# An mLSTM with a channel-mix layer: the hand-ordered list of steps is replaced, with more idle matmuls and a taller spread

## The chip, the cores and the metric

The kernel runs on one core of one Trainium2 chip. The metric is the device time of one execution in microseconds (us). Four compute engines take part: PE (TensorE, matmuls), DVE (VectorE), ACT (ScalarE) and POOL (GpSimd); the SP queue issues every DMA. Each engine works through its own queue strictly in the order in which the program lists its instructions, and waits at an instruction until what it needs is there.

## The reference

There are 4 batches, 8 heads, 768 steps in time and 40 values per head. First an mLSTM recurrence with running maxima `m` as stabilisers runs over the time steps:

```python
m_new = np.maximum(f_gate[:, :, t] + m, i_gate[:, :, t])
f_stab = np.exp(f_gate[:, :, t] + m - m_new); i_stab = np.exp(i_gate[:, :, t] - m_new)
C = f_stab * C + i_stab * (v_t outer k_t);  n = f_stab * n + i_stab * k_t
y[t] = sigmoid(o_gate[t]) * (C @ q_t) / max(|n . q_t|, 1)
```

The heads are then joined to x (4 x 768 x 320), and a channel mix follows, with a shift by one step in time:

```python
xk = mu_k * x + (1 - mu_k) * x_prev;  xr = mu_r * x + (1 - mu_r) * x_prev
out = sigmoid(xr @ w_r) * (np.maximum(xk @ w_k, 0)**2 @ w_v)     # w_k 320x1024, w_v 1024x320
```

## The kernel before, in words

The time axis is cut into 6 chunks of 128 steps, and two batches make a pair. One chunk of one pair is a unit; there are 12 units (u = 0 to 11, chunk u // 2), each with two halves i (one per batch). The recurrence is worked in its chunked form: inside a chunk as a masked attention, between chunks by the state C.

For one half of a unit: `scores` (L268, 16 matmuls) gives k.q in PSUM; `exps` (L257, ACT, four per call) makes the decay weights e; `weigh` (L273, DVE) multiplies the two; `carry_in` (L279) scales k for the state; `attend` (L313, PE) multiplies with v and with the old state; `carry_add` (L323, L325, DVE) updates C; `norm` (L335, L337, L339, three small DVE instructions called den), `gate` (L344) and `outcome` (L350) make x; `twin`, `turn` (L362, PE) and `turned` (L369, ACT) turn it so that channels lie on rows. Then for the whole unit: `change` and `mix` (L377, L383) form the shifted mixtures, `mix_h` and `mix_l` (L392, L398) split them into a rounded part and a remainder, `ffn_k` (L457, four calls of 16 matmuls), `relu`, `square`, `square_h`, `square_l` (L463 to L484), `ffn_r` (L491) and `ffn_v` (L513) do the products, and `result` and `store` finish.

The exponents need, for a given step in time, the running maximum of each head in all 128 rows. For chunk 0 that is done by PE: `spread` (L229 to L233) first adds the causal mask (a 128-row bf16 matmul of 512 columns), and then for each of four heads multiplies a column of the identity, repeated, with the 32 rows (4 batches x 8 heads) of maxima; two such banks per half, four halves for units 0 and 1. For later chunks a DMA does it (`fetch_m`).

The weights arrive as 64-bit floats in 19 pieces (8 of w_k, 3 of w_r, 8 of w_v). For each piece: `load_w` (DMA into one of three stage buffers), `size` (L418, ACT), `bits` steps 0 to 2 (L425, L427, L429, all on DVE), `parts` (the rounded part, mostly ACT, L435) and `parts_l` (the remainder, L441, DVE or POOL). A stage buffer is free again after `bits` step 2. So the first part of the run carries two things at once: the conversion of 19 pieces and the first units.

`warm(n)` (L101) issues n idle bf16 matmuls of 128 rows and 512 columns on constant data; nothing reads them, and they wait for nothing but the fill of ones at the start. Since each engine keeps to its queue, a `warm` delays the PE work listed behind it.

All of these steps are written out one after the other in a list (from L523 on), with the engine as an argument where there is a choice (V = DVE, G = POOL, A = ACT, SY = SP's queue). The list fixes the order on every engine. A planner made it beforehand; in the file it is only the list.

Of the kernel before, what the change touches and what calls it, by code (L numbers as in the profile page):

```python
# [8 lines left out]
F32 = mybir.dt.float32  # L9
# [30 lines left out]
def mlstm_cmix_kernel(ctx: ExitStack, tc, kq, vk, og, gi, gf, wk, wr, wv, mu, pad, out):  # L40
# [556 lines left out]
    bits("wk", 4, 2)
    carry_in(0, 0, V)
    load_o(0, SY)
    spread(1, 0)  # L600
    weigh(0, 1, 0)
    weigh(0, 1, 1)
    attend(0, 0)
    norm(0, 0, 0)
    attend(0, 1)
    parts("wk", 2, A)
    load_w("wk", 6, SY)
    norm(0, 0, 1)
# [5 lines left out]
    gate(0, 0, V)
    norm(0, 1, 0)
    size("wk", 6)
    parts("wk", 4, A)
    zero_state(0, G)
    bits("wk", 6, 0)
    exps(1, 0, 1)  # L620
    carry_add(0, 0)
    size("wr", 0)
    norm(0, 1, 1)
    norm(0, 1, 2)
    parts_l("wk", 4, G)
    spread(1, 1)
# [21 lines left out]
    scores(1, 1)
    weigh(1, 0, 0)
    weigh(1, 0, 1)  # L650
    parts("wr", 0, A)
    load_v(1, SY)
    carry_in(1, 0, V)
    change(0, 0, G)
# [5 lines left out]
    attend(1, 0)  # L660
    fetch_m(2, 0, SY)
    mask(2, 0)
    weigh(1, 1, 1)
    load_o(1, SY)
    parts_l("wr", 0, V)
# [36 lines left out]
    parts_l("wv", 1, G)
    square(0, 0, A)
    load_w("wv", 2, SY)
    bits("wr", 1, 1)
    size("wv", 2)
    carry_in(1, 1, G)
    bits("wr", 1, 2)
    parts("wr", 1, A)
    square_l(0, 0, V)  # L710
    attend(1, 1)
    fetch_m(2, 1, SY)
    bits("wv", 2, 0)
    bits("wv", 2, 1)
    bits("wv", 2, 2)
    load_w("wr", 2, SY)
    mask(2, 1)
    exps(2, 0, 0)
    weigh(2, 0, 0)
    relu(0, 3)  # L720
    norm(1, 1, 0)
    ffn_k(0, 2)
    norm(1, 1, 1)
    size("wr", 2)
    norm(1, 1, 2)
    bits("wr", 2, 0)
    bits("wr", 2, 1)
    bits("wr", 2, 2)
    parts_l("wr", 1, V)
    ffn_k(0, 1)  # L730
    square_h(0, 3, A)
    mix_h(0, "r")
    parts("wv", 2, A)
    parts("wr", 2, A)
    square(0, 3, A)
    mix_l(0, "r", V)
# [20 lines left out]
    ffn_r(0, 1)
    turn(1, 0)
    turned(1, 0)
    load_w("wv", 5, SY)  # L760
    bits("wv", 3, 0)
    load_w("wv", 7, SY)
    bits("wv", 3, 1)
    bits("wv", 3, 2)
    parts("wv", 3, A)
    square(0, 2, A)
    load_w("wv", 4, SY)
    gate(1, 1, V)
# [19 lines left out]
    parts("wv", 5, A)
    parts_l("wv", 5, V)
    parts("wv", 4, A)  # L790
    ffn_v(0, 0, 0, 1)
    load_v(2, SY)
    twin(1, 1, G)
    turn(1, 1)
    ffn_v(0, 1, 0, 1)
    turned(1, 1)
# [5 lines left out]
    fetch_g(2, 1, SY)
    bits("wv", 7, 1)
    bits("wv", 7, 2)
    zeros(1, SY)
    parts("wv", 7, A)
    queries(2, 0, V)
    load_v(3, SY)
    carry_in(2, 0, V)
    ffn_v(0, 0, 1, 2)  # L810
    exps(2, 1, 1)
    ffn_v(0, 0, 2, 3)
    bits("wv", 6, 0)
    bits("wv", 6, 1)
    bits("wv", 6, 2)
    parts("wv", 6, A)
    parts_l("wv", 6, G)
    load_s(3, SY)
    change(1, 0, V)
    change(1, 1, V)  # L820
    mix(1, "k")
# [1017 lines left out]
```

## Time and profile before

| | |
|---|---|
| median of 3 runs | 343.21 us (341.57 to 343.29) |
| the profiled execution | 342.23 us, of it 340.4 us from the first to the last instruction |
| PE busy | 323.1 us (95%) |
| DVE busy | 263.2 us (77%) |
| ACT busy | 223.3 us (66%) |
| POOL busy | 105.5 us (31%) |
| mean granted PE clock | 0.964 of full |

Busy time of PE is modelled (matmuls overlap), so two matmuls' lengths add up to more than the time between their starts. Where a price per matmul is needed, it is better to subtract starts. The granted clock has two levels, 1.2 GHz (0.50) and 2.4 GHz (1.00). The column shows 1.00 until the first change that the trace records, between 32 and 33 us; the lengths of like instructions tell more.

### The profile page before, as it was taken

What the parts mean: (1) busy time and instruction counts of PE and PEld (TensorE: products, weight loads), DVE (VectorE), ACT (ScalarE), POOL (GpSimd) and SP (SyncE); (2) the same over time, 40 slices, a digit from 0 to 9 for tenths busy, and PEclk for the clock granted to TensorE, in tenths of its full rate; (3) what the DMA queues carried; (4) which work ended last, traced back from release to release, by engine and by line L of the source; (5) the groups of instructions that cost most, each with busy time, mean ns of one, the idle gap of its engine ahead of it and who ended that gap; (6) DMA issues with size and microseconds to landing.
All of it is one profiled execution on the core that took longest, in us unless ns stands there. A gap on an engine that the chain in (4) does not pass through costs nothing.

```text
span 340.4 us, 8826 instructions
## 1 busy us (share of the span) xinstructions
PE 323.1 (95%) x3504; PEld 303.4 (89%) x3504; DVE 263.2 (77%) x576; ACT 223.3 (66%) x488; POOL 105.5 (31%) x129
## 2 busy tenths in 40 slices
PE   6999995977999999999999999999999999999996
PEld 3877785867999998999999989999999999999995
DVE  6596999898799977899578798679798776665432
ACT  3756588665788737936969457785776776734442
POOL 2333321121053227162235342556317062320030
PEclk9999598795999999999999999999999999999999
DMA  6749536970370694172945644582668044010011
GB/s 224 241 145 264 168 117 213 274 229 12 95 194 14 183 239 146 44 238 67 244 126 166 189 132 135 141 224 85 154 188 242 5 144 155 3 40 0 2 39 39
DMA packets 25440, 47.29 MB, mean 139 GB/s; under 512 B 2632, under 2 KB 16264, under 8 KB 24440
## 3 DMA queue, kind: packets, MB, share of 16 engines
q1 hardware_dynamic: 25400, 46.74, 47.0%
q8 instruction: 27, 0.44, 0.6%
q14 instruction: 13, 0.11, 0.1%
HBM read 42.63 MB, written 4.10 MB: 137 GB/s over the span
## 4 chain that ended last, share of the span: by engine, by line
PE 54%; DVE 19%; DMA 7%; ACT 4%; issue 2%; SPq 1%; DVEq 0%; ACTq 0%
PE pk L457 18%; PE pv L513 17%; PE pI L313 7%; PE pr L491 6%; PE pS L268 4%; DVE xm L383 4%; DMA vk_sb<-vk 3%; DMA g<-eg 3%; DVE e L273 2%; PE pT L362 1%; DMA wst<-wv 1%; DVE g L246 1%; DVE wf L429 1%; DVE x L354 1%; DVE wf L427 1%
## 5 line engine op out<-in xcount | busy, mean ns | idle before, releaser
L457 PE MATMUL pk<-xlk,wkh 128*128 128x256 f32 x288 | 76.5, 282 | 0.6 <-DVE xlk L398 0.6
L513 PE MATMUL pv<-wvl,kh 128*128 128x320 f32 x192 | 60.2, 313 | 3.7 <-DVE wvl L441 2.8
L513 PE MATMUL pv<-wvh,kh 128*128 128x320 f32 x192 | 61.6, 321 | 0.4 <-ACT wvh L435 0.4
L513 PE MATMUL pv<-wvh,kl 128*128 128x320 f32 x192 | 60.3, 314 | 0.3 <-DVE kl L484 0.2
L463 ACT ACTIVATE rl<-pk 128x512 f32<-128x512 f32 x48 | 28.3, 590 | 42.9 <-PE pk L457 42.6
L457 PEld LDWEIGHTS pk<-xlk,wkh 128*128 128x128 f32 x288 | 55.0, 191 | 1.0 <-DVE xlk L398 1.0
L457 PE MATMUL pk<-xhk,wkh 128*128 128x256 f32 x192 | 55.4, 288 | 0.0
L457 PE MATMUL pk<-xhk,wkl 128*128 128x256 f32 x192 | 53.9, 281 | 0.0
L257 ACT ACTIVATE e<-e,acol 128x128 f32<-128x128 f32 x160 | 50.4, 389 | 1.9 <-POOL e L221 1.7
L273 DVE TENSOR_TENSOR e<-pS,e 128x512 f32<-128x512 f32 x48 | 32.0, 683 | 12.3 <-PE pS L268 10.8
L513 PEld LDWEIGHTS pv<-wvl,kh 128*128 128x128 f32 x192 | 36.5, 190 | 4.5 <-DVE wvl L441 3.4
L383 DVE SCALAR_TENSOR_TENSOR xm<-xd,mu_sb,xT 128x256 f32<-128x256 f32 x72 | 37.3, 575 | 3.6 <-POOL xd L377 3.2
L513 PEld LDWEIGHTS pv<-wvh,kh 128*128 128x128 f32 x192 | 36.4, 190 | 1.5 <-ACT wvh L435 0.8
L513 PEld LDWEIGHTS pv<-wvh,kl 128*128 128x128 f32 x192 | 36.5, 190 | 1.3 <-DVE kl L484 0.9
L457 PEld LDWEIGHTS pk<-xhk,wkh 128*128 128x128 f32 x192 | 36.9, 192 | 0.3
L457 PEld LDWEIGHTS pk<-xhk,wkl 128*128 128x128 f32 x192 | 36.8, 191 | 0.0
L221 POOL TENSOR_SCALAR_AFFINE_SELECT e<-e 128x1024 f32<-128x1024 f32 x20 | 25.5, 1277 | 34.9 <-DMA e<-nm 34.8
L479 DVE CAST kh<-kk 128x512 fp32r<-128x512 f32 x44 | 21.1, 483 | 16.9 <-ACT kk L469 16.8
L469 ACT ACTIVATE kk<-rl 128x512 f32<-128x512 f32 x48 | 29.7, 628 | 1.7 <-DVE kl L484 0.5
L268 PE MATMUL pS<-kq 40*128 40x128 f32 x384 | 30.2, 308 | 0.0
L313 PE MATMUL pI<-vk_sb,e 128*64 128x41 f32 x768 | 29.6, 241 | 0.5 <-DVE e L273 0.5
L313 PEld LDWEIGHTS pI<-vk_sb,e 128*64 128x64 f32 x768 | 26.8, 149 | 3.3 <-issue 1.2
(114 smaller groups left out, 692.9 us busy)
## 6 DMA issues: line engine op xcount, KB each, us to landing
e<-nm SPq DMA_DIRECT2D x20, 512.0 KB
vk_sb<-vk SPq DMA_DIRECT2D x12, 648.0 KB
kq<-kq SPq DMA_DIRECT2D x24, 320.0 KB
g<-eg SPq DMA_DIRECT2D x40, 128.0 KB
sg<-og SPq DMA_DIRECT2D x12, 320.0 KB
out<-sg SPq DMA_DIRECT2D x24, 160.0 KB
wst<-wk SPq DMA_DIRECT2D x8, 384.0 KB
wst<-wv SPq DMA_DIRECT2D x8, 320.0 KB
```

The lines of the kernel that those rows point to most:

```text
L221: G.affine_select(e, e, pattern=[[0, H], [1, L]], compare_op=ALU.is_ge, fill=NEG, base=0, channel_multiplier=-1)
L257: A.activation(e[:, h, :], src, AF.Exp, bias=acol[:, cc, b * H + h:b * H + h + 1])
L268: T.matmul(pS[j][:, p * L:(p + 1) * L], kq2[rw, 0, p, cs], kq2[rw, 1, p, cs], start=True, stop=True)
L273: V.tensor_tensor(ev, t["S", i, half].rearrange("p (h t) -> p h t", h=HH), ev, op=ALU.mult)
L313: T.matmul(*m, start=n < 2, stop=n >= len(mms) - 2, skip_group_check=True)
L383: V.scalar_tensor_tensor(xm[:, ct, :].rearrange("p (b t) -> p b t", b=NB), t["xd"][:, ct], mu_sb[:, "kr".index(nm), ct:ct + 1], xT[u % G2] ...
L457: T.matmul(pk[:, i * U:(i + 1) * U], ww[:, 2 * pr + i, ct * P:(ct + 1) * P], xx[:, ct, :], start=n == 0, stop=n == len(tl) - 1)
L463: A.activation(r, t["pk", pr], AF.Relu)
L469: A.activation(kk, t["r", pr], AF.Square)
L479: eng.tensor_copy(kh, t["kk", pr])
L491: T.matmul(pr[:, :DM], xx[:, ct, i * P:(i + 1) * P], ww[:, ct, :], start=m == 0, stop=m == len(tl) - 1)
L513: T.matmul(t["pv", i][:, :DM], xx[:, ts], ww[:, f, :], start=f == 0 and n == 0, stop=f == NF - 1 and n == 2)
```

## The change

Two helpers change. The tile that holds the maxima of chunk 0 grows from 32 to 128 rows, of which rows 32 to 127 are set to zero by POOL; `spread` then multiplies a column of the whole identity with all 128 rows. What it adds up is the same. Second, the list of steps is new from the first line to the last. The same steps are in it, except for `warm`: 26 calls with 44 idle matmuls in place of 2 calls with 12. 81 steps change engine between DVE and POOL: 43 go to POOL, 38 to DVE.

```diff
-        ar = p2.tile([BH, 3, L], F32, name="ar")
+        ar = p2.tile([P if c == 0 else BH, 3, L], F32, name="ar")
+        if c == 0:
+            G.memset(ar[BH:64, 1, :], 0.0)
+            G.memset(ar[64:P, 1, :], 0.0)
+            ar, full = ar[:BH], ar
...
-            r["i"] = gi_sb[:, r["s"]]
+            r["i"], r["full"] = gi_sb[:, r["s"]], full[:, 1, :]
...
-                T.matmul(pM[:, h * L:(h + 1) * L], ident[:BH, r:r + 1].broadcast_to([BH, P]), rows[0]["ar"][:, 1, :],
+                T.matmul(pM[:, h * L:(h + 1) * L], ident[:, r:r + 1].broadcast_to([P, P]), rows[0]["full"],
                          start=False, stop=h == HH - 1)
```

The new list up to the end of the weight conversion, cut to what the prediction speaks of (numbers are positions in the list; the engine argument is kept):

```
0 constants()   1 begin()   2 gate_b(0)   3 zero_state(0, G)   4 gate_m(0)
5-8 warm(2) x4   9 load_w("wk", 5, SY)   ...   15 columns(0)   ...
24-35 bits("wk", 5|0|1, ...), parts("wk", 5, V)   37 spread(0, 1)   ...   43 spread(0, 0)
44 exps(0, 0, 0)   45 scores(0, 0)   48-51 warm(2) x4   55 weigh(0, 0, 0)   ...
63, 71, 75, 76 warm(2)   67 weigh(0, 0, 1)   70 carry_in(0, 0, V)   77 attend(0, 0)
84 scores(0, 1)   86 spread(1, 0)   96 attend(0, 1)   99 spread(1, 1)   127 turn(0, 0)
131 scores(1, 0)   136 scores(1, 1)   142 turn(0, 1)
144-158 warm, 16 matmuls   160 attend(1, 0)   162-178 bits("wv", 1, ...), bits("wk", 7, ...)
166 gain(1, SY)   167 fetch_g(2, 0, SY)   168 load_w("wr", 1, SY)   179 norm(1, 0, 0)
205 ffn_k(0, 3)   226 ffn_k(0, 0)   241 ffn_k(0, 1)   248 ffn_k(0, 2)   257, 265 ffn_r(0, ...)
253-303 load_w / size of w_v pieces 3, 5, 6, 4, 7   322 parts_l("wv", 7, V)   323 mix_l(1, "k", V)
333, 334, 337 ffn_v(0, ...)   338 ffn_k(1, 0)   ...
```

In the old list, for comparison, `warm(4)` stands at 11 and `warm(8)` at 142, `attend(0, 0)` at 77, `turn(0, 1)` at 120, `attend(1, 0)` at 134, `norm(1, 0, 0)` at 140, `ffn_k(0, 0)` at 143, the `bits` of w_k 7 and w_v 1 between 146 and 160, `parts_l("wv", 7, V)` at 299, `mix_l(1, "k", V)` at 302 and the last two `ffn_v(0, ...)` at 308 and 313.

## Rows read from the trace of the kernel before

**Rows 1.** Page, part 1: busy time, share of span, instructions.

```profile
span 340.4 us, 8826 instructions
PE 323.1 (95%) x3504; PEld 303.4 (89%) x3504; DVE 263.2 (77%) x576; ACT 223.3 (66%) x488; POOL 105.5 (31%) x129
```

**Rows 2.** Timeline of PE, 0 to 88 us: start, length, line, tiles, count.

```profile
1.05 1.89 PE L101 MATMUL pW<-fill 128*128 128x512 bf16 x4 [1.05 <-DVE fill L72]
...
4.98 0.61 PE L229 MATMUL pM<-later,ident_b 128*128 128x512 bf16 x1
5.52 2.07 PE L232 MATMUL pM<-ar,ident 32*128 32x128 f32 x8
7.52 0.61 PE L229 MATMUL pM<-later,ident_b 128*128 128x512 bf16 x1
...
25.02 1.94 PE L313 MATMUL pI<-vk_sb,e 128*64 128x41 f32 x32
...
31.02 0.39 PE L229 MATMUL pM<-later,ident_b 128*128 128x512 bf16 x1
31.34 1.15 PE L232 MATMUL pM<-ar,ident 32*128 32x128 f32 x8
...
33.14 0.88 PE L362 MATMUL pT<-ident,x 128*128 128x128 f32 x3 [0.65 <-DVE x L350]
...
36.95 2.08 PE L268 MATMUL pS<-kq 40*128 40x128 f32 x16
38.96 1.94 PE L313 MATMUL pI<-vk_sb,e 128*64 128x41 f32 x32
...
47.72 1.16 PE L268 MATMUL pS<-kq 40*128 40x128 f32 x16
```

**Rows 3.** Windows: from:to length, busy us (instructions) by engine, granted clock, DMA.

```profile
13.40:17.40 4.00, 4.00 (x27) 3.55 (x27) 0.15 (x2) 2.46 (x8) 0.00 (x0) 1.00 0.82 255
17.40:25.00 7.60, 7.60 (x38) 6.01 (x37) 7.39 (x13) 4.23 (x12) 2.60 (x3) 1.00 0.43 133
41.80:79.00 37.20, 29.12 (x279) 24.80 (x277) 34.93 (x77) 26.83 (x61) 7.42 (x8) 0.87 0.62 191
79.00:85.00 6.00, 6.00 (x29) 6.00 (x30) 4.93 (x13) 2.94 (x4) 0.00 (x0) 0.58 0.03 10
85.00:337.30 252.30, 249.52 (x2903) 242.53 (x2901) 191.02 (x415) 169.73 (x363) 85.66 (x95) 1.00 0.43 123
```

**Rows 4.** Waits of DVE, 0 to 79 us: total, times, longest.

```profile
DVE e L273 <- PE pS L268: 3.9, 1, 3.9
DVE den L335 <- PE pI L313: 2.5, 2, 1.8
DVE wf L425 <- ACT wf L418: 1.2, 1, 1.2
```

**Rows 5.** Waits of PE, 79 to 340 us.

```profile
PE pv L513 <- DVE wvl L441: 2.8, 1, 2.8
```

**Rows 6.** Timeline of DVE, 0 to 88 us.

```profile
17.32 1.29 DVE L273 TENSOR_TENSOR e<-pS,e 128x512 f32<-128x512 f32 x2 [3.85 <-PE pS L268]
...
24.09 0.49 DVE L279 TENSOR_TENSOR kt<-vk_sb,gk 128x320 f32<-128x320 f32 x1
...
37.26 1.20 DVE L279 TENSOR_TENSOR kt<-vk_sb,gk 128x320 f32<-128x320 f32 x1
...
41.82 0.16 DVE L335 TENSOR_SCALAR den<-pI 128x8 f32<-128x8 f32 x1
...
42.76 0.35 DVE L425 TENSOR_SCALAR wf<-wf 128x384 int32<-128x384 int32 x1
...
43.74 0.56 DVE L429 SCALAR_TENSOR_TENSOR wf<-wst,wf 128x384 int32<-128x384 int32 x1
...
78.46 0.48 DVE L441 TENSOR_TENSOR wvl<-wf,wvh 128x320 fp32r<-128x320 f32 x1
```

**Rows 7.** Timeline of POOL, 0 to 88 us.

```profile
37.03 1.09 POOL L221 TENSOR_SCALAR_AFFINE_SELECT e<-e 128x1024 f32<-128x1024 f32 x1
```

More of the change, by code (lines that the diff above doesn't have):

```diff
@@ L606, in mlstm_cmix_kernel @@
+    sigmoid_o(1)
     parts("wk", 2, A)
     load_w("wk", 6, SY)
-    norm(0, 0, 1)
-    norm(0, 0, 2)
-    exps(1, 0, 0)
-    sigmoid_o(0)
-    parts_l("wk", 2, V)
-    load_w("wr", 0, SY)
[L614 to L619, printed above, removed]
-    exps(1, 0, 1)
[L621 to L626, printed above, removed]
+    size("wk", 6)
+    weigh(0, 1, 1)
+    attend(0, 1)
@@ L627, in mlstm_cmix_kernel @@
+    parts("wk", 4, A)
+    carry_add(0, 0)
+    spread(1, 1)
+    parts_l("wk", 2, G)
+    load_o(0, SY)
+    sigmoid_o(0)
+    gate(0, 0, V)
+    exps(1, 0, 0)
+    bits("wk", 6, 0)
+    load_v(1, SY)
+    carry_in(1, 0, V)
+    bits("wk", 6, 1)
+    norm(0, 1, 0)
+    norm(0, 1, 1)
+    parts_l("wk", 4, G)
+    carry_in(1, 1, G)
+    outcome(0, 0, V)
+    norm(0, 1, 2)
+    load_w("wr", 0, SY)
+    size("wr", 0)
+    bits("wr", 0, 0)
+    exps(1, 0, 1)
+    twin(0, 0, V)
     exps(1, 1, 0)
-    bits("wk", 6, 1)
+    bits("wr", 0, 1)
@@ L644, in mlstm_cmix_kernel @@
+    turned(0, 0)
+    load_mu(SY)
     outcome(0, 1, V)
+    weigh(1, 0, 1)
     twin(0, 1, G)
     turn(0, 1)
-    turned(0, 1)
[L648 to L654, printed above, removed]
-    change(0, 1, V)
-    load_mu(SY)
+    size("wv", 1)
+    warm(2)
+    warm(2)
+    weigh(1, 0, 0)
+    mask(2, 0)
+    warm(2)
+    warm(2)
+    load_w("wk", 7, SY)
+    warm(2)
+    warm(2)
+    warm(1)
+    change(0, 0, G)
@@ L657, in mlstm_cmix_kernel @@
+    warm(1)
+    weigh(1, 1, 1)
+    warm(1)
+    warm(1)
+    load_s(2, SY)
+    attend(1, 0)
+    weigh(1, 1, 0)
+    bits("wv", 1, 0)
+    warm(1)
+    turned(0, 1)
+    change(0, 1, V)
+    gain(1, SY)
+    fetch_g(2, 0, SY)
+    load_w("wr", 1, SY)
+    bits("wv", 1, 1)
+    size("wk", 7)
+    bits("wk", 7, 0)
     mix(0, "k")
-    weigh(1, 1, 0)
     mix_h(0, "k")
[L660 to L665, printed above, removed]
+    warm(1)
@@ L700, in mlstm_cmix_kernel @@
     bits("wr", 1, 0)
+    twin(1, 0, V)
+    bits("wr", 1, 1)
+    load_w("wv", 2, SY)
+    size("wv", 2)
+    bits("wv", 2, 0)
+    ffn_k(0, 3)
+    relu(0, 3)
+    bits("wr", 1, 2)
+    attend(1, 1)
+    norm(1, 1, 0)
+    square_h(0, 3, A)
+    weigh(2, 0, 0)
+    norm(1, 1, 1)
+    square(0, 3, A)
+    fetch_m(2, 1, SY)
+    mask(2, 1)
+    norm(1, 1, 2)
+    bits("wv", 2, 1)
+    turn(1, 0)
+    load_w("wr", 2, SY)
+    size("wr", 2)
+    bits("wr", 2, 0)
+    turned(1, 0)
+    bits("wv", 2, 2)
@@ L701, in mlstm_cmix_kernel @@
+    zeros(0, SY)
+    gate(1, 1, V)
+    ffn_k(0, 0)
+    bits("wr", 2, 1)
+    mix_h(0, "r")
+    mix_l(0, "r", V)
+    parts("wr", 1, A)
+    parts_l("wr", 1, V)
+    parts("wv", 2, A)
+    relu(0, 0)
+    load_v(2, SY)
     square_h(0, 0, A)
-    parts_l("wv", 1, G)
+    bits("wr", 2, 2)
+    parts_l("wv", 2, V)
     square(0, 0, A)
[L704 to L736, printed above, removed]
@@ L753, in mlstm_cmix_kernel @@
-    fetch_g(2, 0, SY)
-    twin(1, 0, V)
-    parts("wv", 0, A)
-    ffn_r(0, 0)
[L757 to L768, printed above, removed]
+    bits("wv", 0, 2)
+    square_l(0, 3, V)
+    load_w("wv", 3, SY)
+    load_w("wv", 5, SY)
+    size("wv", 3)
+    bits("wv", 3, 0)
+    ffn_r(0, 0)
     outcome(1, 1, V)
@@ L783, in mlstm_cmix_kernel @@
     bits("wv", 4, 1)
+    carry_in(2, 0, V)
     bits("wv", 4, 2)
-    scores(2, 1)
+    bits("wv", 6, 2)
     size("wv", 7)
+    fetch_m(3, 0, SY)
+    parts("wv", 4, A)
     bits("wv", 7, 0)
[L788 to L796, printed above, removed]
+    load_v(3, SY)
+    attend(2, 0)
     parts_l("wv", 4, V)
-    ffn_v(0, 1, 1, 2)
-    load_w("wv", 6, SY)
-    size("wv", 6)
+    bits("wv", 7, 1)
@@ L801, in mlstm_cmix_kernel @@
+    parts("wv", 6, A)
     square_l(0, 2, V)
[L802 to L821, printed above, removed]
     ffn_v(0, 1, 2, 3)
     exps(2, 1, 0)
-    weigh(2, 1, 0)
+    bits("wv", 7, 2)
@@ L907, in mlstm_cmix_kernel @@
     norm(2, 1, 2)
+    square_h(1, 2, V)
+    turn(2, 0)
     gate(2, 1, V)
+    carry_old(2, 1, G)
+    carry_add(2, 1)
     outcome(2, 1, V)
+    carry_old(3, 0, G)
+    twin(2, 1, V)
+    carry_in(3, 0, V)
+    ffn_v(1, 1, 1, 2)
+    gate_m(3)
+    zeros(1, SY)
     ffn_v(1, 0, 0, 1)
-    weigh(3, 0, 0)
-    twin(2, 1, G)
-    carry_add(2, 1)
-    weigh(3, 0, 1)
     ffn_v(1, 0, 1, 2)
-    sigmoid(1)
+    fetch_g(3, 0, SY)
     turned(2, 0)
+    change(2, 0, V)
     turn(2, 1)
-    fetch_g(3, 0, SY)
@@ L997, in mlstm_cmix_kernel @@
-    twin(3, 1, V)
-    scale_k(4, V)
-    turn(3, 1)
-    exps(4, 0, 1)
-    square(2, 2, A)
-    square_h(2, 2, V)
-    mask(4, 1)
+    square_l(2, 0, V)
+    ffn_k(2, 3)
+    relu(2, 3)
+    square_h(2, 1, V)
+    square_l(2, 1, G)
+    ffn_k(2, 2)
+    relu(2, 2)
+    square(2, 2, A)
+    outcome(3, 0, V)
+    exps(4, 1, 0)
+    carry_in(3, 1, V)
+    ffn_v(2, 1, 0, 1)
+    attend(3, 1)
+    square(2, 3, A)
+    twin(3, 0, V)
+    store(1, 0, SY)
+    norm(3, 1, 0)
+    scores(4, 1)
+    norm(3, 1, 1)
@@ L1021, in mlstm_cmix_kernel @@
+    ffn_v(2, 0, 0, 1)
+    gain(2, SY)
+    fetch_g(4, 0, SY)
+    gate_b(4)
+    gate_i(4, G)
+    load_v(4, SY)
+    twin(3, 1, V)
+    ffn_v(2, 1, 1, 2)
+    turn(3, 1)
+    mask(4, 0)
+    weigh(4, 1, 0)
+    exps(4, 0, 1)
+    ffn_v(2, 0, 1, 2)
+    square_l(2, 2, V)
+    ffn_v(2, 0, 2, 3)
+    square_h(2, 3, V)
+    square_l(2, 3, V)
+    gate_m(4)
+    scale_a(4, V)
     turned(3, 0)
     change(3, 0, V)
+    exps(4, 0, 0)
+    weigh(4, 0, 0)
+    fetch_g(4, 1, SY)
+    turned(3, 1)
     change(3, 1, G)
-    mix(3, "r")
+    gate_r(4)
@@ L1041, in mlstm_cmix_kernel @@
-    logits(2, 1)
     logits(2, 0)
     sigmoid(2)
+    columns(3)
+    weigh(4, 0, 1)
+    attend(4, 0)
+    mix_l(3, "k", V)
+    ffn_k(3, 1)
+    relu(3, 1)
+    square(3, 1, A)
+    ffn_k(3, 0)
+    mix(3, "r")
+    load_s(5, SY)
+    mix_h(3, "r")
+    carry_in(5, 1, V)
+    relu(3, 0)
+    norm(4, 0, 0)
     fetch_m(5, 1, SY)
     norm(4, 0, 1)
+    gain(3, SY)
     norm(4, 0, 2)
-    ffn_v(2, 0, 3, 4)
-    result(2, 1)
-    gate(4, 0, G)
-    carry_add(4, 0)
-    mix_h(3, "r")
-    ffn_k(3, 1)
@@ L1173, in mlstm_cmix_kernel @@
+    queries(6, 0, V)
+    outcome(5, 0, V)
+    ffn_v(3, 1, 3, 4)
+    gain(5, SY)
+    mask(6, 1)
     square_h(4, 1, V)
     square_l(4, 1, V)
-    ffn_k(4, 2)
     relu(4, 2)
-    ffn_k(4, 3)
+    square(4, 2, A)
+    twin(5, 1, G)
     turn(5, 1)
-    exps(6, 0, 1)
+    turned(5, 1)
+    result(3, 0)
+    twin(5, 0, G)
+    turn(5, 0)
+    scores(6, 1)
+    turned(5, 0)
+    square_h(4, 0, V)
+    square_l(4, 0, G)
+    exps(6, 1, 0)
+    fetch_g(6, 1, SY)
+    square_h(4, 2, V)
+    scores(6, 0)
@@ L1199, in mlstm_cmix_kernel @@
-    fetch_m(6, 1, SY)
-    mask(6, 1)
-    exps(6, 1, 0)
-    weigh(6, 0, 1)
-    fetch_m(7, 0, SY)
-    mask(7, 0)
-    exps(7, 0, 1)
-    change(5, 1, G)
-    mix(5, "k")
-    scores(6, 1)
-    weigh(6, 1, 0)
-    columns(4)
-    attend(6, 0)
-    mix(5, "r")
-    queries(6, 1, V)
-    norm(6, 0, 0)
-    mix_h(5, "k")
-    mix_l(5, "k", V)
+    weigh(6, 1, 0)
+    square_l(4, 2, V)
+    weigh(6, 0, 1)
+    ffn_v(4, 1, 2, 3)
+    weigh(6, 1, 1)
+    carry_in(6, 0, V)
+    change(5, 0, G)
+    change(5, 1, V)
@@ L1218, in mlstm_cmix_kernel @@
     ffn_v(4, 0, 1, 2)
+    ffn_k(5, 0)
+    relu(5, 0)
+    norm(6, 1, 2)
+    gate(6, 1, V)
+    mix(5, "r")
+    mix_h(5, "r")
+    carry_old(6, 0, G)
+    ffn_v(4, 1, 3, 4)
+    outcome(6, 1, V)
+    carry_add(6, 0)
+    twin(6, 1, V)
+    square(5, 0, A)
+    ffn_k(5, 1)
+    relu(5, 1)
+    turn(6, 1)
+    store(3, 1, SY)
+    turned(6, 1)
+    ffn_v(4, 0, 2, 3)
+    ffn_v(4, 0, 3, 4)
+    square(5, 1, A)
+    square_h(5, 0, V)
+    square_l(5, 0, V)
+    carry_old(7, 0, G)
+    load_v(7, SY)
@@ L1379, in mlstm_cmix_kernel @@
-    relu(6, 3)
-    outcome(7, 1, V)
-    twin(7, 1, G)
+    load_v(9, SY)
+    fetch_g(8, 0, SY)
+    queries(8, 0, V)
+    ffn_v(6, 0, 0, 1)
+    ffn_v(6, 0, 1, 2)
+    square(6, 3, A)
+    ffn_v(6, 1, 1, 2)
+    ffn_v(6, 1, 2, 3)
+    mask(9, 0)
+    mix(7, "r")
+    carry_add(7, 1)
+    exps(9, 0, 1)
+    mix(7, "k")
+    square_h(6, 3, V)
+    square_l(6, 3, G)
+    fetch_g(8, 1, SY)
+    scores(8, 1)
+    queries(8, 1, V)
     load_s(9, SY)
-    turn(7, 1)
+    scores(9, 0)
+    carry_in(8, 0, V)
@@ L1469, in mlstm_cmix_kernel @@
+    load_o(9, SY)
+    ffn_k(7, 2)
+    exps(9, 1, 1)
+    square_h(7, 0, V)
+    relu(7, 2)
+    square(7, 1, A)
+    result(6, 0)
+    square_l(7, 0, V)
+    ffn_v(7, 1, 0, 1)
+    weigh(9, 0, 1)
+    store(6, 0, SY)
+    change(8, 0, V)
+    change(8, 1, V)
+    mix(8, "r")
     ffn_r(7, 1)
@@ new lines, in mlstm_cmix_kernel @@
+    ffn_k(9, 0)
+    square_h(8, 3, V)
+    fetch_g(11, 0, SY)
+    queries(11, 0, V)
+    fetch_m(11, 0, SY)
+    mask(11, 0)
+    exps(11, 0, 1)
+    weigh(11, 0, 1)
+    mix_l(9, "r", V)
+    square_l(8, 3, G)
+    ffn_v(8, 1, 3, 4)
+    result(8, 1)
+    exps(11, 0, 0)
+    weigh(11, 0, 0)
+    ffn_v(8, 0, 3, 4)
+    gate(10, 1, G)
+    outcome(10, 1, V)
+    ffn_k(9, 2)
+    twin(10, 1, V)
+    turn(10, 1)
+    relu(9, 0)
+    square(9, 0, A)
+    square_h(9, 0, V)
+    turned(10, 1)
+    square_l(9, 0, V)
```

1473 lines of the change are left out of this document (688 added, 785 removed).

## The prediction

> **What bounds the kernel now.** I began with the page's busy times: PE is busy for 323 of 340.4 us [rows 1], which looks like a kernel with nothing left. The windows correct that. From 85.0 to 337.3 us PE is busy 249.5 of 252.3 us at the upper clock level [rows 3]: this part is bound by PE, and no order of steps can take more than the 2.8 us of holes out of it. The first 79 us are another matter. The last long wait of PE there is for a remainder of a w_v piece, 2.8 us [rows 5]; it comes from DVE at 78.46 us [rows 6], and between 41.8 and 79.0 us DVE is busy 34.9 of 37.2 us while PE has holes [rows 3]. So the sum is: the time at which DVE has converted the last weights, plus 258.3 us of PE work (79.0 to 337.3), plus the tail to 340.4 and the 1.8 us around the span. Whatever brings that DVE instruction forward brings the end forward by as much.
>
> Why does DVE get there only at 78.46? It waits 3.9 us for the first scores and 2.5 us for the first attention products, both from PE [rows 4]. PE was not idle in those waits: it is busy without a hole from 13.4 to 25.0 us [rows 3], but slow. A bank of `spread` takes 2.54 us early on (starts 4.98 and 7.52) and 0.32 + 1.15 = 1.47 us at 31.02; 16 score matmuls take 2.01 us at 36.95 (to the next start) and 1.16 at 47.72 [rows 2]. So PE ran at its lower level, 1.2 GHz, up to 29 us, although the clock column shows 1.00 there [rows 3]; like instructions settle it. The first fast rows come behind a stretch of 128-row matmuls from 25.02 us on (`attend`); the 32-row and 40-row matmuls before it kept PE busy and the level stayed low. The same is seen again at 38.96 and at 79.0: the level rises some microseconds into 128-row work.
>
> The Trainium skill (TensorE: Matmul & The Clock Gate, "Part 1: The HAM clock gate") has it that the gate opens for an engine that has been busy for a while, and says nothing of the height of the matmuls. By that sentence the gapless 11.6 us from 13.4 on, of 32-row and 40-row work, would have raised the level, and rows of zeros added below would change nothing. Here the trace disagrees, since PE stayed slow through it; so I give the page's reading only the chance of the slow rival below, where the taller spread leaves the level where it was.
>
> **The change, part by part.** (1) *The taller spread.* 64 matmuls become 128 rows tall. The trace has no such form. From above, the 128-row transposes of 128 f32 columns, 0.27 us each at the lower level (33.14 to 33.94, three), against 0.25 for a 32-row spread matmul (5.52 to 7.52, eight) [rows 2]: 64 x 0.02 = 1.3 us of PE. From below 0. I take 0, since the number of columns is the same. The POOL memsets lie before anything waits for POOL. What it may give is the clock, in (3).
>
> The Trainium skill (same page, "LDWEIGHTS (loading the stationary operand)") says that a weight load is timed by its columns, not its rows; no run here shows that for this form yet.
>
> (2) *Idle matmuls.* 44 instead of 12. One costs 1.89 / 4 = 0.47 us at the lower level [rows 2], and about half, 0.22, at the upper. Eight stand at the front, while PE has nothing else until the first maxima are there (before, it had a hole there): nothing. Sixteen are listed after `scores(0, 0)`, before `attend(0, 0)`: 3.5 us of PE at the upper level in a wait for DVE. Sixteen more stand between `turn(0, 1)` and `attend(1, 0)`, and these are on a path, see (4).
>
> (3) *Up to attend(0, 0).* Before, it starts at 25.02 [rows 2]. With 128-row work from 1 us on I expect the upper level somewhere between 5 and 10 us; then `spread` and `scores` are through by 12 to 15 us, the scores are ready when DVE comes to them, and the 3.85 us wait goes. DVE also has less to do before: the new list does one `bits` step of piece 2, the three of piece 4, two `weigh` and two memsets later or elsewhere. Three `bits` are about 1.4 us (0.35, 0.56, 0.56, less the overlap; starts 42.76 and 43.74), the two `weigh` 1.2 (17.32) [rows 6], with the fourth `bits` and memsets 3.7 in all; against it come one `carry_in` and two remainders, 1.3. So 2.4 us less, and `attend(0, 0)` starts at 25.0 - 3.9 - 2.4 = 18.7.
>
> (4) *From there to norm(1, 0, 0)*, DVE's first look at unit 1, 41.82 before [rows 6]. At the upper level PE has to do, in its order: two `attend` (1.4 each), two `spread` halves of two banks (2.9 each), three `scores` (1.0), two `turn` (0.3): 12.2 us, as much as DVE has in that stretch; then 16 idle matmuls 3.5 and `attend(1, 0)` 1.4. That is 18.7 + 17.1 = 35.8. What is gained so far: 6.0 us.
>
> (5) *From norm(1, 0, 0) to the last remainder.* Before: 78.46 - 41.82 = 36.6 us. The new list has the `bits` of w_k 7 and w_v 1 (2 x 1.3) and some of POOL's former share behind it already; against that come three DVE remainders and a twin: net 2.6 us less. 36.6 - 2.6 = 34.0; arrival at 69.8, gain 8.7 us.
>
> (6) *What takes some back.* The new order has narrower places. `fetch_g(2, 0)` stands on SP's queue right behind `gain(1)`, whose write it must see, and the load of w_r 1 and all later pieces wait behind both. The last w_v pieces (6, 4, 7) can only be loaded when `bits` of the piece three before has been done, some 4 to 5 us of DVE work ahead of their use; one such wait was 1.2 us before [rows 4]. And 43 steps went to POOL, 38 came from it: a DVE instruction that meets POOL work takes 1.20 instead of 0.49 us (`carry_in` at 37.26, beside the mask at 37.03) [rows 6, 7]. Bounds: 0, and 6 us, the size of the gain up to (4). I take 3, between them, since two waits like the old 1.2 are about that.
>
> (7) *From then on* the PE work is the same, so 258.3 us, including some 2.5 us at the lower level up to 84 us (0.58 of full over 6.0 us [rows 3]), which I keep, because PE again has holes before. The 2.8 us of later holes could go or double: I take no change. ACT loads its tables twice less; ACT has idle time throughout: 0.
>
> Sum: 342.2 (profiled execution, 340.4 + 1.8) - 8.7 + 3.0 = 336.5. The median shown, 343.2, lies 1 us above that execution, within the spread of the three runs; I leave the forecast at 336.5.
>
> **Rivals.** *A. The gain comes, and goes again behind 79 us* (0.18). The start gains 6 us, but then DVE becomes the late engine: its list work up to `ffn_v(1, 0, ...)` is within 1 us of what it was for the same PE work, so PE, 6 us ahead, meets DVE again and again. For: before, DVE was busy 191 of 252 us in that stretch [rows 3], three quarters on the mean and more near its beginning. Against: holes of only 2.8 us. If holes grow by 4 us: 340.5.
>
> *B. Slower: the level stays low until the idle block at 144* (0.14). If zeros do not help, spread, scores, turns and attends of (4) cost about 22 us: two spreads 10.2, three scores 6, two attends 4.6, two turns 1.6. `attend(0, 0)` then starts near 21.5 (no 3.9 us gain), `turn(0, 1)` ends at 43, and the 16 idle matmuls stand before `attend(1, 0)` with 0.47 us each, at least until the level rises: about 6 us. norm(1, 0, 0) comes at 50.5 instead of 41.8; with 34.0 us after it the remainder is at 84.5, 6 us late: 348. It decides when that block takes over 5 us with PE behind. For: 32-row data in a sea of zeros is an odd way to raise a clock. Against: 24 idle 128-row matmuls come before, and mask matmuls too.
>
> *C. Better* (0.12): the holes of (6) don't come, and the level is up when the last weights arrive: 336.5 - 3 - 2.5 = 331.
>
> **Chances.** The forecast has 0.56, with its own range 333.5 to 339.5. Within 0.5% (about what a measurement of this kernel can tell from no change) means 341.5 to 344.9. Faster: 0.56, C 0.12, and a little under half of A, without what lies over 341.5 in the forecast's tail: 0.74 in all. Same: half of A and a bit of the tail: 0.12. Slower: B: 0.14. Range for 8 of 10: 330 to 343.
>
> **What would show it.** Right: in the new trace a spread bank takes 1.4 to 1.5 us, not 2.5, by its second or third half; the 3.9 us wait of DVE for the first scores is gone; `attend(0, 0)` at 17 to 20, norm(1, 0, 0) at 34 to 38, the last w_v remainder at 67 to 75 us; holes of PE from there on within 2 us of 2.8. Wrong: a low level up to the idle block (B), or a last remainder that is early while the end is not (A), or new waits of DVE for `size` above 3 us in sum (6).

## The result, and the profile after

The changed kernel takes 333.98 us (median of 4 runs, 329.28 to 340.3) against 342.79 for the kernel before (median of 4); the ratio is 0.966, 95% interval 0.957 to 0.975. In a later series beside the kernel before it took 333.72 us (median of 6), 0.975 (0.971 to 0.978). Medians here are over all runs and ratios over those within 1.5% of the kernel's fastest, which leaves out two of the four, and two of the six, one of them of 760.48 us. The medians alone give 0.974 and 0.977. The kernel before keeps within 1.7 us; the changed one does not, which plays a part below.

The profiled execution took 329.28 us, 327.5 of it in the span. Page, part 1, of the changed kernel (answers to [rows 1]):

```profile
span 327.5 us, 8897 instructions
PE 313.6 (96%) x3536; PEld 293.0 (89%) x3536; DVE 248.5 (76%) x571; ACT 219.4 (67%) x486; POOL 111.7 (34%) x136
```

DVE has 571 instructions instead of 576 and is busy 15 us less; POOL has 136 instead of 129. The timeline of PE (start, length, line, tiles, count), answering to [rows 2]:

```profile
1.05 3.60 PE L101 MATMUL pW<-fill 128*128 128x512 bf16 x8 [1.05 <-DVE fill L72]
...
4.91 0.39 PE L233 MATMUL pM<-later,ident_b 128*128 128x512 bf16 x1
5.13 1.05 PE L236 MATMUL pM<-ar,ident 128*128 128x128 f32 x8
6.03 0.38 PE L233 MATMUL pM<-later,ident_b 128*128 128x512 bf16 x1
...
10.15 0.46 PE L272 MATMUL pS<-kq 40*128 40x128 f32 x2 [0.64 <-DMA kq<-kq]
12.02 2.04 PE L272 MATMUL pS<-kq 40*128 40x128 f32 x14 [1.41 <-DMA kq<-kq]
14.00 5.83 PE L101 MATMUL pW<-fill 128*128 128x512 bf16 x16
19.75 1.13 PE L317 MATMUL pI<-vk_sb,e 128*64 128x41 f32 x32
...
33.57 4.60 PE L101 MATMUL pW<-fill 128*128 128x512 bf16 x16
38.10 1.13 PE L317 MATMUL pI<-vk_sb,e 128*64 128x41 f32 x32
```

The eight idle matmuls at the front take 3.60 us, and the first spread bank is at the upper level already: 1.12 us from 4.91 to 6.03, where the kernel before had 2.54. The scores then wait twice for their DMA, 0.64 and 1.41 us, and the level falls: the block of 16 idle matmuls takes 5.8 us from 14.00, not 3.5, and `attend(0, 0)` starts at 19.75. The second block of 16 stands from 33.57 to 38.10.

Timeline of DVE, its first `weigh`, the first look at unit 1 (norm(1, 0, 0)) and the last w_v remainder, which answer to lines of [rows 6]; then the waits of DVE in the first 80 us, which answer to [rows 4]:

```profile
13.78 0.69 DVE L277 TENSOR_TENSOR e<-pS,e 128x512 f32<-128x512 f32 x1 [2.07 <-ACT e L261]
...
39.59 0.17 DVE L339 TENSOR_SCALAR den<-pI 128x8 f32<-128x8 f32 x1 [1.35 <-PE pI L317]
...
69.12 0.48 DVE L445 TENSOR_TENSOR wvl<-wf,wvh 128x320 fp32r<-128x320 f32 x1
```

```profile
DVE den L339 <- PE pI L317: 4.1, 2, 2.7
DVE e L277 <- ACT e L261: 2.3, 2, 2.1
...
DVE wf L429 <- ACT wf L422: 0.8, 2, 0.5
DVE e L277 <- PE pS L272: 0.5, 1, 0.5
```

The remainder comes at 69.12 instead of 78.46 us, 9.3 us earlier. The 3.85 us wait at the first `weigh`, which ended with the scores, has become one of 2.07 us that ends with `exps` on ACT (L261); the 0.5 us wait for scores is a later one, in unit 1. The first look at unit 0's attention products waits 2.7 us, behind the first idle block. The windows around and behind that remainder, answering to [rows 3]:

```profile
39.59:69.60 30.01, 26.49 (x278) 23.25 (x276) 29.08 (x70) 23.28 (x59) 7.09 (x8) 0.94 0.76 230
66.00:69.66 3.66, 3.08 (x14) 2.68 (x12) 3.63 (x6) 2.26 (x5) 1.80 (x2) 0.54 0.91 207
69.66:74.66 5.00, 5.00 (x40) 5.00 (x41) 4.93 (x13) 4.22 (x6) 0.00 (x0) 1.00 0.54 150
69.66:324.30 254.64, 251.74 (x2930) 245.55 (x2930) 189.29 (x423) 171.12 (x365) 93.37 (x100) 1.00 0.42 123
```

From the remainder to its last matmul PE needs 254.6 us (69.66 to 324.30) where the kernel before needed 258.3. There PE ran its first 5 us at 1.2 GHz; here it is back at 2.4 by then. The holes behind 70 us are as small as before:

```profile
PE pT L366 <- DVE C L329: 1.3, 1, 1.3
PE pI L317 <- DVE e L277: 0.8, 2, 0.5
```

So 9.3 us by the earlier remainder and 3.7 behind it make the 12.9 us between the two spans. On the medians the gain is 8.8 us; this execution lies below its median.

### The profile page after: what moved, and what is told of

Same layout as the page of the kernel before. It is cut to its first block, busy times and chain, and to the rows that moved or that the text cites. A ratio compares the mean times of both kernels' runs of the same rounds, so it can differ in the third digit from the quotient of the medians.

```text
span 327.5 us, 8897 instructions
## 1 busy us (share of the span) xinstructions
PE 313.6 (96%) x3536; PEld 293.0 (89%) x3536; DVE 248.5 (76%) x571; ACT 219.4 (67%) x486; POOL 111.7 (34%) x136
## 4 chain that ended last, share of the span: by engine, by line
PE 69%; DVE 12%; DMA 10%; ACT 4%; issue 3%; SPq 1%; POOL 0%; DVEq 0%; POOLq 0%; ACTq 0%
PE pk L461 22%; PE pv L517 19%; PE pI L317 10%; PE pr L495 7%; PE pS L272 5%; PE pW L101 3%; DMA kq<-kq 3%; DMA e<-nm 2%; PE pT L366 2%; DMA wst<-wr 2%; DVE e L277 2%; DMA vk_sb<-vk 2%; ACT e L261 2%; DVE wf L431 2%; DMA g<-eg 2%
## 5 line engine op out<-in xcount | busy, mean ns | idle before, releaser
L461 PE MATMUL pk<-xlk,wkh 128*128 128x256 f32 x288 | 75.4, 278 | 0.0
L461 PE MATMUL pk<-xhk,wkh 128*128 128x256 f32 x192 | 54.4, 283 | 0.0
L461 PEld LDWEIGHTS pk<-xlk,wkh 128*128 128x128 f32 x288 | 54.2, 188 | 0.0
L261 ACT ACTIVATE e<-e,acol 128x128 f32<-128x128 f32 x160 | 50.1, 391 | 2.8 <-POOL e L225 2.6
L488 POOL TENSOR_TENSOR kl<-kk,kh 128x512 fp32r<-128x512 f32 x21 | 32.2, 1537 | 49.6 <-DVE kh L483 44.4
L225 POOL TENSOR_SCALAR_AFFINE_SELECT e<-e 128x1024 f32<-128x1024 f32 x20 | 23.6, 1181 | 51.7 <-DMA e<-nm 41.3
L461 PEld LDWEIGHTS pk<-xhk,wkh 128*128 128x128 f32 x192 | 36.1, 188 | 0.3
L387 DVE SCALAR_TENSOR_TENSOR xm<-xd,mu_sb,xT 128x256 f32<-128x256 f32 x72 | 32.6, 509 | 1.1 <-POOL xd L381 0.9
L272 PE MATMUL pS<-kq 40*128 40x128 f32 x384 | 28.3, 288 | 3.7 <-DMA kq<-kq 2.6
L272 PEld LDWEIGHTS pS<-kq 40*128 40x128 f32 x384 | 24.6, 193 | 6.2 <-ACT e L261 2.2
```

The costliest lines, as they stand in the source:

```text
L225: G.affine_select(e, e, pattern=[[0, H], [1, L]], compare_op=ALU.is_ge, fill=NEG, base=0, channel_multiplier=-1)
L261: A.activation(e[:, h, :], src, AF.Exp, bias=acol[:, cc, b * H + h:b * H + h + 1])
L272: T.matmul(pS[j][:, p * L:(p + 1) * L], kq2[rw, 0, p, cs], kq2[rw, 1, p, cs], start=True, stop=True)
L387: V.scalar_tensor_tensor(xm[:, ct, :].rearrange("p (b t) -> p b t", b=NB), t["xd"][:, ct], mu_sb[:, "kr".index(nm), ct:ct + 1], xT[u % G2] ...
L461: T.matmul(pk[:, i * U:(i + 1) * U], ww[:, 2 * pr + i, ct * P:(ct + 1) * P], xx[:, ct, :], start=n == 0, stop=n == len(tl) - 1)
L488: eng.tensor_tensor(kl, t["kk", pr], t["kh", pr].bitcast(F32), op=ALU.subtract)
```

## The experiments

Three series, each kernel timed beside the kernel before. Ratios are to the kernel before of the same series.

**1. Which of the three parts brings it?** The change has a taller spread, more idle matmuls and a new order. The first four kernels take them apart. *New list and idle matmuls, spread on 32 rows:*

```diff
-ident[:, r:r + 1].broadcast_to([P, P]), rows[0]["full"],
+ident[:BH, r:r + 1].broadcast_to([BH, P]), rows[0]["ar"][:, 1, :],
```

> The new list with all its idle matmuls, the spread back on 32 rows. My theory (the gain is PE's level in the first 30 us, and it needs full-height work to stay up): the eight idle matmuls at the front still raise the level at about 5 us, but it does not hold through four spread halves of 32-row work; some of the eight banks take 2.5 us, attend(0, 0) starts at 21 to 25 instead of 19.75 us, and the time is 336 to 341. Rival 1 (the order alone, the level is of no account): 329 to 334, as the changed kernel. Rival 2 (the idle matmuls alone hold the level): all spread banks 1.1 to 1.5 us, 329 to 334.

Measured: 337.67 us, 0.984 (0.978 to 0.989). Its PE timeline:

```profile
1.05 3.60 PE L101 MATMUL pW<-fill 128*128 128x512 bf16 x8 [1.05 <-DVE fill L72]
...
5.17 1.15 PE L236 MATMUL pM<-ar,ident 32*128 32x128 f32 x8
6.58 1.15 PE L236 MATMUL pM<-ar,ident 32*128 32x128 f32 x8
7.98 1.98 PE L236 MATMUL pM<-ar,ident 32*128 32x128 f32 x8
10.43 2.07 PE L236 MATMUL pM<-ar,ident 32*128 32x128 f32 x8
...
38.17 5.63 PE L101 MATMUL pW<-fill 128*128 128x512 bf16 x16
```

Two banks at the upper level, then the lower one again, though PE has no hole there; the idle block before `attend(1, 0)` now ends at 43.7. As my theory had it, and against both rivals; only `attend(0, 0)` starts at 20.06 us, sooner than the 21 to 25 that I expected.

*New list, tall spread, no idle matmuls at all:*

```diff
-    warm(2)     # and the 25 other calls
```

> The new list with the 128-row spread and no idle matmul at all. My theory: PE begins with the spread at about 4.6 us at the lower level, which rises some way through it; then PE has holes up to the second unit and falls back; unit 1 is worked at the lower level and the time is 336 to 341. Rival 1 (order alone): 329 to 334. A third reading (the idle matmuls stand in PE's way, since DVE waited 2.7 and 1.35 us behind two blocks of 16): below the changed kernel, 326 to 330.

Measured: 329.64 us, 0.964 (0.959 to 0.968). My theory of that moment was wrong: nothing is lost. The spread needs no help, as its timeline shows:

```profile
5.30 1.92 PE L236 MATMUL pM<-ar,ident 128*128 128x128 f32 x8
7.43 1.91 PE L236 MATMUL pM<-ar,ident 128*128 128x128 f32 x8
9.56 1.54 PE L236 MATMUL pM<-ar,ident 128*128 128x128 f32 x8
11.16 1.05 PE L236 MATMUL pM<-ar,ident 128*128 128x128 f32 x8
```

It starts at the lower level and rises to the upper one in its third bank. That is some 5 us later than with the front block. DVE comes to the first scores at 12.2 us and waits 2.2 us for them, where the front-only kernel below waits 0.8 us; the times of the two do not show this difference.

*The new list alone* (both edits):

> The new list alone: spread on 32 rows, no idle matmuls. My theory: PE stays at the lower level until the first long run of 128-row work, DVE waits for scores as in the kernel before, and the time is 339 to 346, that is, at most a third of the gain is left. Rival 1 (order alone): 329 to 334.

Measured: 339.39 us (334.75 to 342.39), 0.985 (0.979 to 0.991): by the ratio about two fifths of the gain is left, more than the third that I gave it. The medians (339.39 against 341.22 for the kernel before) leave only a sixth, so the size of this part is uncertain; rival 1 (329 to 334) is out either way. With experiment 1 (0.984) it says that the idle matmuls do nothing for a 32-row spread.

*The tall spread in the old list, with its 12 idle matmuls:*

```diff
-        ar = p2.tile([BH, 3, L], F32, name="ar")
+        ar = p2.tile([P if c == 0 else BH, 3, L], F32, name="ar")     # zeros below, as in the change
...
+ident[:, r:r + 1].broadcast_to([P, P]), rows[0]["full"],
```

> The old list with its 12 idle matmuls, only the spread on 128 rows. My theory: the level rises within the first four spread banks (by 10 us), the 3.9 us wait of DVE for the first scores shrinks below 1.5 us, and the time falls by 2 to 5 us, to 338 to 341. Rival 1 (order alone): no change, 342 to 343. If full height does nothing for the level: no change either, and the banks stay at 2.5 us.

Measured: 334.8 us, 0.980 (0.977 to 0.983): 6.4 us, more than I expected. DVE no longer waits for the first scores in its trace. Its spread on PE, and its last remainder on DVE:

```profile
5.44 1.91 PE L236 MATMUL pM<-ar,ident 128*128 128x128 f32 x8
7.57 1.39 PE L236 MATMUL pM<-ar,ident 128*128 128x128 f32 x8
9.01 1.05 PE L236 MATMUL pM<-ar,ident 128*128 128x128 f32 x8
```

```profile
72.15 0.48 DVE L445 TENSOR_TENSOR wvl<-wf,wvh 128x320 fp32r<-128x320 f32 x1
```

The two ratios multiply: 0.980 x 0.985 = 0.965, and both together, without idle matmuls, gave 0.964. By the medians the order is worth 1.8 us with the short spread (341.22 to 339.39) and 5.2 us with the tall one (334.8 to 329.64). So the gain by the tall spread is shown on its own, the order adds a second one that is clearest beside the tall spread, and the idle matmuls are no third. What in the new order brings its part was not taken apart.

Nor does a run part the level from the form of the spread. A tall bank is shorter at the lower level too (2.13 against 2.54 us, see step 1 below); an estimate from these rows is that four such banks before the first scores would take 4 x 0.41 = 1.6 us off the 3.85 us wait without any rise of the level.

**2. Are the idle matmuls in the way?** *The changed kernel once more*, as partner:

> The changed kernel once more, unedited, as the partner of the other kernels of this series: 328 to 337 us, a ratio of 0.96 to 0.98 to the kernel before.

Measured: 333.72 us, 0.975 (0.971 to 0.978).

*Only the eight at the front:*

```diff
     gate_m(0)
     warm(2)  x4
...
-    warm(2)     # and all the later ones: 48 to 76, 144 to 190
```

> The changed kernel with only the eight idle matmuls at the front, without the two blocks of 16 and the four single places behind. Theory now: the tall spread raises and holds PE's level, and the two blocks only stand before attend(0, 0) and attend(1, 0), where DVE waited 2.7 and 1.35 us. Then those two waits shrink below 1.5 us in sum, norm(1, 0, 0) is at 36 to 38.5 instead of 39.6 us, and the time is 2 to 4 us below the changed kernel of the same series; the front block gives the early spread banks the upper level (1.1 us each from the first). Rival (the blocks hold the level for unit 0's feed-forward): 2 us or more above it.

Measured: 328.69 us, 0.959 (0.956 to 0.963), 5 us below its partner and the intervals apart. It beats both kernels. In its trace `attend(0, 0)` begins at 15.23 (and, held by its second half of weights, goes on at 16.55) instead of 19.75, `attend(1, 0)` at 32.36 instead of 38.10, and norm(1, 0, 0) comes at 37.73 instead of 39.59:

```profile
15.23 0.45 PE L317 MATMUL pI<-vk_sb,e 128*64 128x41 f32 x4 [2.13 <-DMA vk_sb<-vk]
16.55 1.72 PE L317 MATMUL pI<-vk_sb,e 128*64 128x41 f32 x28 [0.87 <-DVE e L277]
...
32.36 1.13 PE L317 MATMUL pI<-vk_sb,e 128*64 128x41 f32 x32
```

```profile
37.73 0.16 DVE L339 TENSOR_SCALAR den<-pI 128x8 f32<-128x8 f32 x1
```

The last remainder is no earlier in that execution (69.45). DVE, sooner at unit 1, now waits for `size` of later weight pieces, 4.2 us in the first 80 us instead of 0.8:

```profile
DVE wf L429 <- ACT wf L422: 4.2, 5, 2.6
```

The profiled executions of the two kernels are only 0.7 us apart (328.57 and 329.28). So the blocks' cost, with that of the four single idle matmuls, is shown in the medians and in unit 1, and not followed to the end.

*No idle matmul, again:*

> The changed kernel without any idle matmul, again, now beside the unedited one: 2 to 4 us below it if the blocks only stand in the way; equal if the gap between the two series was that of chips; within 1 us of the kernel with the front block alone, because DVE doesn't reach the first scores before 12 us either way.

Measured: 330.13 us, 0.964 (0.960 to 0.969), the same ratio as in the first series. Without the blocks the kernel is 3.6 us below its partner; whether the front block adds something cannot be told (the intervals of 0.959 and 0.964 overlap, and a repeat of the front-only kernel below gave 0.965).

*The old list, tall spread, no idle matmuls:*

> The old list with the 128-row spread and without its 12 idle matmuls (beside 334.8 us with them). If the idle matmuls give nothing: 333 to 336. If warm(8) before the first ffn_k is what keeps the level up there: the first ffn_k at the lower level, 336 to 339.

Measured: 335.94 us, 0.982 (0.979 to 0.985), against 0.980 with them: in the time, nothing that can be told. The first `ffn_k` does run at the lower level, as the second reading had it (the granted clock is 0.53 from 36 to 43 us, against 1.00 in the old list with the idle matmuls), but the time doesn't show it.

**3. Does the end hang on DVE's last remainder alone?** The base is the front-only kernel.

> The new list with the tall spread and the eight idle matmuls at the front only, unedited, as the partner of this series: 326 to 331 us, 0.955 to 0.965 of the kernel before.

Measured: 331.4 us, 0.965 (0.960 to 0.969).

*40 small DVE instructions more, before the remainder:*

```diff
+    spare = cp.tile([P, 96], F32, name="spare")
+    def extra(n):
+        for _ in range(n): V.tensor_tensor(spare, spare, spare, op=ALU.mult)
...
             V.scalar_tensor_tensor(wb, p["hi"], -0x80000000, wb, ...)   # bits, step 1
+            if nm == "wv":
+                extra(5)
```

> The partner with 40 more small DVE instructions (128x96 on a spare tile, an estimate of 0.13 to 0.17 us each, 5.2 to 6.8 us in all), five behind bits step 1 of each of the eight w_v pieces, so before the last remainder. My theory (the end is that remainder plus a fixed run of PE work): the remainder and the end are both later by the whole, 4.5 to 7 us. Rival (PE's total work or the DMA sets the end, DVE's early load has slack): under 2 us.

Measured: 340.28 us, 0.993 (0.990 to 0.996), 8.9 us more. Each of the 40 took twice what I had estimated; why was not tested:

```profile
L73 DVE TENSOR_TENSOR spare<-spare 128x96 f32<-128x96 f32 x40 | 12.1, 302 | 1.1
```

```profile
79.05 0.48 DVE L454 TENSOR_TENSOR wvl<-wf,wvh 128x320 fp32r<-128x320 f32 x1
```

The partner's remainder:

```profile
67.58 0.48 DVE L445 TENSOR_TENSOR wvl<-wf,wvh 128x320 fp32r<-128x320 f32 x1
```

12 us of extra work, the remainder 11.5 us later, the medians 8.9 us apart. But PE does not wait for that remainder any more. Its last long wait of the early part, in the partner and here:

```profile
68.12 0.42 PE L517 MATMUL pv<-wvl,kh 128*128 128x320 f32 x1 [1.77 <-DVE wvl L445]
```

```profile
76.88 0.63 PE L526 MATMUL pv<-wvh,kl 128*128 128x320 f32 x1 [3.78 <-DVE kl L497]
```

Here it ends with `square_l` (kl), which stands in DVE's queue right behind the last five extra instructions. It ends 8.8 us later than the partner's, as much as the medians differ. So the delay does pass on to the end, by way of another DVE instruction than my theory had.

*The same 40, in units 4 to 7:*

```diff
         V.tensor_tensor(t["sg"][:, i, :], t["pv", i][:, :DM], t["sg"][:, i, :], op=ALU.mult)   # result
+        if 4 <= u < 8:
+            extra(5)
```

> The partner with the same 40 DVE instructions, five at each result step of units 4 to 7, behind the weight conversion. My theory: PE bounds this part and DVE has slack, so the end moves by less than 1 us. Rival (DVE's total is what counts, wherever it lies): 4.5 to 7 us later.

Measured: 338.64 us, 0.990 (0.987 to 0.992): 7.2 us more. My theory fell here. Work that DVE does long after the remainder costs nearly as much. The extra instructions lie between 178 and 267 us; PE's longest wait comes right behind the last five of them (the second line is PE's waits from 70 us on, then DVE, PE and a window in the layout of [rows 3]):

```profile
L73 DVE TENSOR_TENSOR spare<-spare 128x96 f32<-128x96 f32 x40 | 12.6, 315 | 1.1
```

```profile
PE pI L324 <- DVE e L284: 4.4, 2, 3.9
```

```profile
263.23 3.06 DVE L73 TENSOR_TENSOR spare<-spare 128x96 f32<-128x96 f32 x5
```

```profile
267.63 1.63 PE L324 MATMUL pI<-vk_sb,e 128*64 128x41 f32 x32 [3.88 <-DVE e L284]
```

```profile
265.00:275.00 10.00, 7.37 (x77) 7.21 (x78) 5.72 (x17) 4.33 (x9) 4.67 (x7) 0.83 0.23 79
```

Five of them mostly take 1.4 us; these took 3.06, beside a POOL instruction from 262.46 us on. The `weigh` behind them is 3.9 us late for PE, and the granted clock is 0.83 over 265 to 275 us, so the wait costs again in slow matmuls. That is one place. A wait of 1.0 us with 0.83 behind it, at 115 us, comes before any extra instruction, so the trace shows the path of the 7.2 us only in part. DVE is busy three quarters of that stretch on the mean, but its queue has no slack for the extra work at such a place. The window that the prediction read, PE full and DVE at 76% [rows 3], did not show that; only adding work did.

*11 DVE instructions less before the remainder* (it leaves out the sign of w_v and w_r):

```diff
         elif step == 1 and nm != "wk":
+            pass
```

> The partner without bits step 1 (the sign of the weight) of the eight w_v and the three w_r pieces: 11 DVE instructions of some 0.41 us less, 4.5 us, so the weights of these two matrices are taken without their sign. My theory: the last remainder comes 3 to 4.5 us earlier; the end follows it, unless the loads or PE come due first, which they may, since PE has less room to do its other early work: 2 to 4.5 us less. Rival (slack on DVE): under 1 us.

Measured: 329.61 us, 0.959 (0.955 to 0.963), 1.8 us below its partner with intervals that overlap. So 4.5 us less on DVE brought at most part of itself. In its trace (335.28 us) the last remainder is at 67.3 us, hardly before the partner's 67.58, and DVE waits 6.0 us for `size` instead of 3.6; that suggests that the loads came due first, and doesn't show it.

## Why the prediction was right, point by point

Forecast 336.5, measured 333.98 and 333.72; the mechanism was the one named, and several sizes in it were off, in both directions.

*What bounds the kernel.* Right as far as the first 80 us go: remainder 9.3 us earlier, end 12.9 us earlier in the profiled executions, and work added before it delays the end (though there PE's last wait was for `square_l`). Wrong in "no order of steps can take more than the 2.8 us of holes" as a picture of what lies behind: true of gains, but 12.6 us of extra DVE work there cost 7.2 us.

*Step 1, the price of the tall spread.* My bounds were 0 and +1.3 us; the truth lies outside them, on the good side. A bank takes 2.13 us (5.30 to 7.43, no idle matmuls) where the 32-row one took 2.54 at the same level [rows 2], and 1.12 against 1.41 (5.17 to 6.58 in experiment 1) at the upper: 2.3 to 3.3 us less over eight banks. One taller matmul:

```profile
L236 PEld LDWEIGHTS pM<-ar,ident x64: 190/190/201, 4.9 to 27.9; 128*128 128x128 f32 x64
L236 PE MATMUL pM<-ar,ident x64: 272/275/275, 5.1 to 28.0; 128*128 128x128 f32 x64
```

and in the kernel before, at both levels mixed:

```profile
L232 PE MATMUL pM<-ar,ident x64: 270/416/578, 5.5 to 32.2; 32*128 32x128 f32 x64
```

The length of one at best is the same (272 and 270 ns); it is the row of eight that is shorter.

*The level.* Right that it was low, that it cost, and that the spread is where to raise it. With 32 rows PE fell back to 2.45 us a bank in gapless work (experiment 1), with 128 rows it rose in the third bank without help (experiment 2). The sentence of the Trainium skill (TensorE: Matmul & The Clock Gate, "Part 1: The HAM clock gate") that a busy engine is released does not hold for this 32-row work, as the trace before had already said. The same page's other statement, that a single matmul with 32 rows takes as long as one with 128 ("Why this matters for your kernels"), agrees with the 270 and 272 ns above, but it does not carry over to a whole bank: 1.41 against 1.12 us.

*Step 2, idle matmuls at no cost.* Wrong for the two blocks of 16: without them the kernel is 5 us faster (0.959 against 0.975), and unedited it waits 2.7 and 1.35 us behind them. I had costed the first block at the upper level, 3.5 us, inside a wait for DVE; it ran 5.8 us, and DVE waited for what stood behind it. And the front block, on which my argument against rival B stood, is not needed for the spread to rise.

*Step 3.* 18.7 forecast, 19.75 measured; PE came out of the block only then, and of the 3.85 us wait that I took to go 2.07 us stayed, now for ACT. *Step 4.* 35.8 forecast, 39.59 measured: PE waited 0.53 us for a DMA and 0.55 us for ACT before scores, some of its work ran at the lower level, and the second block took 4.5 instead of 3.5 us. Both forecasts were too low.

*Step 5.* 34.0 us forecast for the stretch to the remainder, 29.5 measured (39.59 to 69.12), the largest miss. The window of the kernel before, the same stretch:

```profile
41.82:78.94 37.12, 29.10 (x278) 24.78 (x276) 34.85 (x77) 26.75 (x61) 7.42 (x8) 0.87 0.63 191
```

The new order has 70 DVE instructions there, not 77, 29.08 us against 34.85, and 0.9 us of holes against 2.3. I had counted 2.6 us of moved work and stretched the rest like the old; but the six `mix` instructions there, 0.96 us each on the mean, take 0.71 now, and `bits` step 2 of the w_v and w_r pieces 0.49 instead of 0.57. *Step 6*, the 3 us given back, did not come in this kernel: one wait for `size` of 0.5 us in that stretch. It comes without the idle blocks, with 4.2 us of such waits in the front-only kernel. So (3) to (6) together: 72.8 forecast for the remainder, with the give-back, 69.12 measured; the misses of 3.8 late and 7.5 early partly cancel, so the nearness of the forecast is in part luck.

*Step 7.* 258.3 forecast, 254.6 measured, as rival C had it: the level is up when the last weights arrive (1.00 against 0.50 in the first 5 us).

*Rivals.* A (the gain goes again behind) did not come; the extra work in units 4 to 7 shows that DVE has little to spare there. B (the level stays low) is refuted by the banks of 1.12 us; with the spread on 32 rows its idle block does stand in the way, and even then the kernel is faster than before. Both conditions of C came; its 331 lies between the profiled execution (329.28) and the median (333.98).

*The signs.* Two of those that I named were missed: a wait of 2.07 us is left at the first `weigh`, and norm(1, 0, 0) at 39.59 lies outside 34 to 38. The others came: the spread bank at the upper level, `attend(0, 0)` at 19.75, the remainder at 69.12, and 2.9 us of holes behind it.

## What to carry to other kernels

Read PE's level from the lengths of like instructions, early in a kernel above all, and try the form of the first matmuls: here zeros added below 32 rows of data were worth 2% in the old order, while 44 idle matmuls were worth nothing in the time and cost 1 to 1.6% where they stood before real work (0.964 and 0.959 without, 0.975 with). An idle matmul is only free in a hole that stays as long as planned. And a wait that a change removes can leave a shorter one behind it, for another engine: look at the instruction, not only at the total by releaser. A busy share of 75% is no proof of slack: before calling an engine off the path, add work to it there and time it.

## What the runs showed of the hardware that I had not expected

A spread bank of 128-row f32 matmuls is faster than one with 32 rows at both levels (1.12 against 1.41 us, 2.13 against 2.54), with single matmuls (272 and 270 ns) and weight loads (190 and 180 ns) nearly alike at best. Why was not tried. In one execution of the changed kernel (760.48 us) a spread bank took 2.97 us, longer than at either level elsewhere, while the clock column read 1.00 throughout; why is open. The new order is less even from run to run than the old: 329 to 340 us in four runs, against 341.6 to 343.3; the old list with the tall spread stays within 2 us (333.78 to 335.77). What makes the new order uneven was not tried.
